# Attention, Hardswish MLP and capacity MoE on one core: Newton steps on GpSimd, output copies on ScalarE, later and denser w_in conversions, the first pair's steps earlier

## The chip, the core and the metric

The kernel runs on one core of a Trainium2 chip (trn2). The metric is the device time in microseconds, as the median of the runs. The engines are TensorE (PE; its weight loads are PEld), VectorE (DVE), ScalarE (ACT), GpSimd (POOL) and SyncE (SP, which here issues the DMAs).

## The reference

Three stages follow one another: attention over 4 batches of 12 heads (448 tokens, head size 64) with RMS-normalised q and k, a Hardswish MLP from 768 to 2048 to 768 over the 1792 tokens, and a mixture of eight experts that fills every expert up to a capacity of 224 tokens.

```python
def rmsnorm(x, g):
    rms = np.sqrt(np.mean(x * x, axis=-1, keepdims=True) + 1e-06)
    return x / rms * g
q_n, k_n = (rmsnorm(q, g_q), rmsnorm(k, g_k))
scores = scale * np.matmul(q_n, k_n.transpose(0, 1, 3, 2))
attn = np.exp(scores - np.max(scores, axis=-1, keepdims=True))
attn_out = np.matmul(attn / (np.sum(attn, axis=-1, keepdims=True) + 1e-09), v)
...
h = x @ w_in                                   # the MLP
x = (h * np.clip(h + 3.0, 0.0, 6.0) / 6.0) @ w_out
...
h = np.maximum(x[mask] @ w1[e], 0.0)           # each of the 8 experts
out[mask] = h @ w2[e]
```

`w_in` and `w_out` come as 64-bit floats; q, k, v and the experts' weights are 32-bit.

## The kernel before

Attention works on pairs of heads, 24 of them, each cut into four chunks of 112 tokens. One pair goes through these functions. `load` and `vload` bring q, k and v. `sums` squares q and k on ACT (`sq`) and adds up the squares on DVE. `invert` turns the mean squares into inverse roots by an integer first guess (lines 240 and 241) and three Newton steps of three small instructions each (lines 243 to 245), all on DVE; it is called once for pair 0, once for pair 1, and from then on once for two pairs together, on tiles of 112x16 or 112x32 elements. `norm` multiplies q and k by the result (`xn`, on GpSimd, but for the very first q). `transp` transposes them on PE and splits them into a high and a low part (`qh`, `ql`, `kh`, `kl`; ACT and DVE). `s1` forms a first score matrix, whose row maxima DVE takes (`mx`); `mt` transposes the maxima, and DVE spreads them (`mr`). `sT` forms the transposed scores by eight matmuls a chunk, and ACT takes exp (`ph`). `av` multiplies with v; at the end of a head DVE reads the row sums (`scol`) and copies the product out of PSUM (`num`, line 374). `normalize` takes the reciprocal on DVE and multiplies on GpSimd (`xq`); `xt` transposes that on PE into the MLP's input (`xh`, `xl`).

In parallel `conv` turns the 64-bit weights into 32-bit ones: one DMA load (`wraw`, two buffers), four DVE instructions over 128x768 elements (`narrow`, lines 134 to 137, into `cv`) and one DMA store, 16 times for `w_in` and 16 times for `w_out`.

The order of all this is written out by hand. Every step gets a place on one scale by `at(t, ...)`, 16 places to a pair, pair i from `t = 16 * i` on; the steps are sorted by place and recorded in that order, and each engine runs its own instructions strictly in that order. So `invert` of a group stands at place 16*g-42, `norm` of pair i at 16*i-38, its transposes at 16*i-30 and 16*i-28, `sT` from 16*i to 16*i+12, `normalize` at 16*i+28 and `xt` at 16*i+33. Between them matmuls of the MLP's first layer (`mlp1_atoms`, line 431) fill PE, from place 117 on, when the first six pairs (batch 0) are through. Its weights are loaded from the converted copy (`win_load`) from place 98 on.

Of the kernel before, what the change touches and what calls it, by code (L numbers as in the profile page):

```python
# [12 lines left out]
AF = mybir.ActivationFunctionType  # L13
OP = mybir.AluOpType
# [7 lines left out]
def kernel(  # L22
# [14 lines left out]
    nc = tc.nc  # L37
# [32 lines left out]
    T_LOAD, T_VLOAD, T_NORM, T_Q, T_K, T_V = -72, -20, -38, -30, -28, 6  # L70
    T_SUMS, T_INV = -50, -42
    T_S1, T_MT = (-24, -20, -16, -12), -7
    T_ST = (0, 4, 8, 12)
    T_AV = ((17, 18, 19.5, 20.5), (22, 23, 24.5, 25.5))
    T_NUM, T_XT, T_MLP = 28, 33, 37
    T_CI, D_CI, T_CO, D_CO, T_CL = 4, 11, 180, 12, 14


    order = ExitStack()
# [158 lines left out]
    def invert(g):  # L238
        ms, y, t = ST[g]
        nc.vector.tensor_scalar(ms, ms, 1.0 / D, 1e-6, op0=OP.mult, op1=OP.add)  # L240
        nc.vector.tensor_scalar(y.bitcast(I32), ms.bitcast(I32), -0.5, 1597463007.0, op0=OP.mult, op1=OP.add)
        for _ in range(3):
            nc.vector.scalar_tensor_tensor(t, y, -0.5, y, op0=OP.mult, op1=OP.mult)
            nc.vector.tensor_tensor(t, t, ms, op=OP.mult)
            nc.vector.scalar_tensor_tensor(y, t, 1.5, y, op0=OP.add, op1=OP.mult)

    def norm(i):
        g = GROUP[i]
# [85 lines left out]
    def av(i, s, n):  # L334
# [29 lines left out]
        num, sc, _ = NUM[i]  # L364
        m = slice(n - QT + 1, n + 1)
        pv = p[:CP, :QT * W].rearrange("p (n w) -> p n w", w=W)
        if SPLIT:
            x = num[:, m, s]
            nc.vector.tensor_scalar(sc[:, s, m], pv[:, :, 128], eps[:CP], None, op0=OP.add)
            nc.vector.tensor_copy(x, pv[:, :, 0:64])  # L370
            nc.vector.tensor_tensor(x, pv[:, :, 64:128], x, op=OP.add)
        else:
            nc.vector.tensor_scalar(sc[:, s, m], pv[:, :, 64], eps[:CP], None, op0=OP.add)
            nc.vector.tensor_copy(num[:, m, s], pv[:, :, 0:64])

    def normalize(i):
        num, sc, xq = NUM[i]
# [248 lines left out]
    def at(t, fn, *args):  # L626
        events.append((t, len(events), fn, args))
# [6 lines left out]

    for i in range(NH // 2):
        t = 16 * i
        at(t + T_LOAD, load, i)
        at(t + T_VLOAD, vload, i)
        g = GROUP[i]
        first = 16 * g[0]  # L640
        at(first + T_SUMS + 4 * (i - g[0]), sums, i)
        if i == g[-1]:
            at(first + T_INV, invert, g)
        at(t + T_NORM, norm, i)
        at(t + T_Q, transp, i, 0)
        at(t + T_K, transp, i, 1)
        at(t + T_V, vsplit, i)
        for c in range(NCH):
            at(t + (T_S1[c] if i else -24 + c), s1, i, c)
            at(t + T_ST[c], sT, i, c)  # L650
            for s in range(2):
                at(t + T_AV[s][c], av, i, s, c)
        at(t + (T_MT if i else -19), mt, i)
        at(t + T_NUM, normalize, i)
        at(t + T_XT, xt, i)
        if (i + 1) % NP == 0:
            at(t + T_MLP, mlp_next, i // NP)
    at(T_LOAD, load_scales)
# [411 lines left out]
    for pi, (t, hfs) in enumerate(passes):  # L1070
# [10 lines left out]
        for f in range(NF):  # L1081
            i, k = divmod(f, QF)
# [139 lines left out]
```

## Time and profile before

| what | value |
|---|---|
| median of 3 runs | 1244.47 us (1239.93 to 1245.07) |
| the profiled execution | 1238.81 us, its span 1237.0 us |
| busy in the span: PE, DVE, ACT, POOL | 1177.1, 807.7, 529.1, 408.2 us |
| mean granted clock of TensorE | 0.98 of full speed |

The profile is of one execution. Busy times of an engine count its instructions; "PEclk" is the clock granted to TensorE in a stretch, 1.00 being 2.4 GHz and 0.50 being 1.2 GHz. A timeline row gives start, duration, engine, line, operation and tiles; in square brackets stands the idle time of the engine ahead of it and what ended that.

### The profile page before, as it was taken

What the parts mean: (1) busy time and instruction counts of PE and PEld (TensorE: products, weight loads), DVE (VectorE), ACT (ScalarE), POOL (GpSimd) and SP (SyncE); (2) the same over time, 40 slices, a digit from 0 to 9 for tenths busy, and PEclk for the clock granted to TensorE, in tenths of its full rate; (3) what the DMA queues carried; (4) which work ended last, traced back from release to release, by engine and by line L of the source; (5) the groups of instructions that cost most, each with busy time, mean ns of one, the idle gap of its engine ahead of it and who ended that gap; (6) DMA issues with size and microseconds to landing.
All of it is one profiled execution on the core that took longest, in us unless ns stands there. A gap on an engine that the chain in (4) does not pass through costs nothing.

```text
span 1237.0 us, 21103 instructions
## 1 busy us (share of the span) xinstructions
PE 1177.1 (95%) x7952; PEld 1008.8 (82%) x7952; DVE 807.7 (65%) x1726; ACT 529.1 (43%) x971; POOL 408.2 (33%) x293
## 2 busy tenths in 40 slices
PE   3899999999999999998998999999998899999997
PEld 2778888888888888887776877777777799999997
DVE  7987967767767866435885466666667565555550
ACT  3543544444454454444773211111112466555650
POOL 2211222223222321012453222222234567666641
PEclk9886999999999999999999999999999899999999
DMA  5563775564554655427986422222234788787731
GB/s 140 151 178 112 198 216 168 164 188 156 179 194 137 194 158 183 145 74 212 325 292 194 119 65 69 64 78 61 71 84 125 220 248 250 238 244 239 227 116 45
DMA packets 221750, 201.69 MB, mean 163 GB/s; under 512 B 19152, under 2 KB 200912, under 8 KB 221648
## 3 DMA queue, kind: packets, MB, share of 16 engines
q1 hardware_dynamic: 218320, 189.33, 51.1%
q0 software_dynamic: 3328, 11.01, 2.9%
q8 instruction: 62, 1.02, 0.3%
q14 instruction: 40, 0.33, 0.1%
HBM read 162.03 MB, written 38.27 MB: 162 GB/s over the span
## 4 chain that ended last, share of the span: by engine, by line
PE 74%; DVE 8%; issue 5%; DMA 3%; POOL 1%; ACT 1%; SPq 0%; POOLq 0%; DVEq 0%; ACTq 0%
PE h L431 17%; PE y L1026 16%; PE av L358 11%; PE y L1174 8%; PE st L318 6%; PE h L1110 5%; PE h L1112 2%; PE rt L837 2%; PE t L273 1%; DVE C L832 1%; PE s L296 1%; DMA gr<-g_dr 1%; DMA we_s<-in_moe_w_dram 1%; PE t L390 1%; PE h L562 1%
## 5 line engine op out<-in xcount | busy, mean ns | idle before, releaser
L358 PEld LDWEIGHTS av<-vv,ph 112*112 112x112 f32 x1536 | 178.6, 186 | 12.5 <-issue 8.5
L358 PE MATMUL av<-vv,ph 112*112 112x66 f32 x1536 | 183.3, 267 | 0.0
L329 ACT ACTIVATE ph<-st 112x448 f32<-112x448 f32 x192 | 93.8, 541 | 140.0 <-PE st L318 139.7
L431 PE MATMUL h<-xh,wh 128*128 128x448 f32 x384 | 152.6, 397 | 0.0
L970 POOL TENSOR_TENSOR g2l<-gr,g2h 128x512 fp32r<-128x512 f32 x60 | 78.7, 1313 | 209.1 <-ACT g2h L968 157.3
L431 PE MATMUL h<-xh,wl 128*128 128x448 f32 x384 | 142.5, 371 | 0.0
L299 DVE TENSOR_REDUCE mx<-s 112x1 f32<-112x448 f32 x192 | 109.3, 612 | 50.7 <-PE s L296 50.6
L431 PE MATMUL h<-xl,wh 128*128 128x448 f32 x384 | 142.1, 370 | 0.0
L112 POOL TENSOR_TENSOR wel<-we_s,weh 128x768 fp32r<-128x768 f32 x60 | 120.6, 2015 | 57.8 <-ACT weh L111 46.3
L112 DVE TENSOR_TENSOR wel<-we_s,weh 128x768 fp32r<-128x768 f32 x68 | 90.2, 1334 | 69.6 <-ACT weh L111 59.3
L111 ACT ACTIVATE weh<-we_s 128x768 fp32r<-128x768 f32 x128 | 105.8, 841 | 69.3 <-DMA we_s<-in_moe_w_dram 51.3
L112 POOL TENSOR_TENSOR wl<-win_v,wh 128x768 fp32r<-128x768 f32 x32 | 60.9, 1903 | 223.3 <-ACT wh L111 209.7
L1026 PE MATMUL y<-woh,g2l 128*128 128x512 f32 (+1 forms) x448 | 128.7, 348 | 1.0 <-POOL g2l L970 1.0
L1026 PE MATMUL y<-woh,g2h 128*128 128x512 f32 (+1 forms) x448 | 127.3, 347 | 0.0
L968 ACT ACTIVATE g2h<-gr 128x512 fp32r<-128x512 f32 x60 | 37.9, 631 | 209.0 <-PE y L1026 159.3
L1026 PE MATMUL y<-wol,g2h 128*128 128x512 f32 (+1 forms) x448 | 126.4, 346 | 0.0
L1110 PE MATMUL h<-xe,weh 128*128 128x448 f32 x384 | 121.1, 377 | 2.2 <-DVE xe L1061 2.2
L1112 PE MATMUL h<-xe,wel 128*128 128x224 f32 x384 | 92.8, 269 | 0.0
L1174 PE MATMUL y<-weh,hl 128*112 128x384 f32 x256 | 86.4, 338 | 0.0
L1174 PE MATMUL y<-weh,hh 128*112 128x384 f32 x256 | 86.3, 337 | 0.0
L1174 PE MATMUL y<-wel,hh 128*112 128x384 f32 x256 | 86.3, 337 | 0.0
L431 PEld LDWEIGHTS h<-xh,wh 128*128 128x128 f32 x384 | 72.5, 189 | 13.3 <-issue 8.3
(235 smaller groups left out, 2386.2 us busy)
## 6 DMA issues: line engine op xcount, KB each, us to landing
we_s<-in_moe_w_dram SPq DMA_DIRECT2D x128, 384.0 KB, 4.4
win_v<-w SPq DMA_DIRECT2D x64, 384.0 KB, 3.9
g_dr<-g SPq DMA_DIRECT2D x64, 224.0 KB, 2.9
gr<-g_dr SPq DMA_DIRECT2D x52, 256.0 KB, 2.9
wraw<-in_moe_w_in_dram SPq DMA_DIRECT2D x16, 768.0 KB, 6.9
wraw<-in_moe_w_out_dram SPq DMA_DIRECT2D x16, 768.0 KB, 7.1
gr<-g_dr SPq DMA_DIRECT2D x48, 224.0 KB, 4.2
w<-cv SPq DMA_DIRECT2D x16, 384.0 KB, 3.1
```

Source lines behind the costliest of these rows:

```text
L111: nc.scalar.activation(hi, raw, AF.Copy)
L112: eng.tensor_tensor(lo, raw, hi.bitcast(F32), op=OP.subtract)
L299: mx = nc.vector.tensor_reduce(MX[i][:, s, c:c + 1], pp[s][:CP, :S], axis=AX.X, op=OP.max)
L318: nc.tensor.matmul(pp[s][:CP, :S], a[r], b[r], start=(n == 0), stop=(n == len(todo) - 1))
L329: nc.scalar.activation(e, pp[s][:CP, :S], AF.Exp)
L358: nc.tensor.matmul(p[:CP, o:o + W], PP[i, s, c][0][:, qs], vv[:, s, c, 64:], start=(c == 0), stop=(c == NCH - 1))
L431: nc.tensor.matmul(p[:, :S], w[:, c], x[:, c], start=(n == 0), stop=(n == 3 * NC - 1))
L970: eng.tensor_tensor(gl, g, gh.bitcast(F32), op=OP.subtract)
L1026: nc.tensor.matmul(pp[hf][:, :COLS[hf].stop - COLS[hf].start], a[:, f % QF], w[:, COLS[hf]], start=(f == 0 and n == 0), stop=(f == NF - 1 ...
L1110: mm = [lambda: nc.tensor.matmul(p[:, :4 * CP], wh[:, fo], x.rearrange("d k t -> d (k t)"), start=(c == 0), stop=(c == NC - 1), skip_group ...
L1112: lambda: nc.tensor.matmul(p[:, :2 * CP], wl[:, fo], x[:, 0], start=False, stop=False, skip_group_check=True)]
L1174: nc.tensor.matmul(p[:CP, :HW], a[:, f, tk], w[:, o], start=(f == 0 and n == 0), stop=(f == FB - 1 and n == 2))
```

## The change

Four things are changed.

1. In `invert` the Newton steps leave DVE for GpSimd. DVE keeps the two instructions of the first guess. GpSimd first multiplies the mean squares by -0.5, and a step is four instructions there instead of three: 1 + 3 x 4 = 13 in place of 9.
2. The copy of the product out of PSUM (`num`) goes from DVE to ACT.
3. The `w_in` conversions start at place 36 instead of 4, and stand 9 places apart instead of 11.
4. For pair 0 alone, `vload`, `vsplit`, `sT`, `av`, `normalize` and `xt` stand 17 places earlier.

```diff
-    T_CI, D_CI, T_CO, D_CO, T_CL = 4, 11, 180, 12, 14
+    T_CI, D_CI, T_CO, D_CO, T_CL = 36, 9, 180, 12, 14
...
         nc.vector.tensor_scalar(y.bitcast(I32), ms.bitcast(I32), -0.5, 1597463007.0, op0=OP.mult, op1=OP.add)
+        nc.gpsimd.tensor_scalar(ms, ms, -0.5, None, op0=OP.mult)
         for _ in range(3):
-            nc.vector.scalar_tensor_tensor(t, y, -0.5, y, op0=OP.mult, op1=OP.mult)
-            nc.vector.tensor_tensor(t, t, ms, op=OP.mult)
-            nc.vector.scalar_tensor_tensor(y, t, 1.5, y, op0=OP.add, op1=OP.mult)
+            nc.gpsimd.tensor_tensor(t, y, y, op=OP.mult)
+            nc.gpsimd.tensor_tensor(t, t, ms, op=OP.mult)
+            nc.gpsimd.tensor_scalar(t, t, 1.5, None, op0=OP.add)
+            nc.gpsimd.tensor_tensor(y, y, t, op=OP.mult)
...
-            nc.vector.tensor_copy(num[:, m, s], pv[:, :, 0:64])
+            nc.scalar.activation(num[:, m, s], pv[:, :, 0:64], AF.Copy)
...
         t = 16 * i
+
+        u = t if i else t - 17
         at(t + T_LOAD, load, i)
-        at(t + T_VLOAD, vload, i)
+        at(u + T_VLOAD, vload, i)
...
-        at(t + T_V, vsplit, i)
+        at(u + T_V, vsplit, i)
...
-            at(t + T_ST[c], sT, i, c)
+            at(u + T_ST[c], sT, i, c)
             for s in range(2):
-                at(t + T_AV[s][c], av, i, s, c)
+                at(u + T_AV[s][c], av, i, s, c)
         at(t + (T_MT if i else -19), mt, i)
-        at(t + T_NUM, normalize, i)
-        at(t + T_XT, xt, i)
+        at(u + T_NUM, normalize, i)
+        at(u + T_XT, xt, i)
```

On PE, from the transpose of pair 0's maxima on (`t<-ident,mx`), before, `st` being the transposed scores, `s` the first scores and `t<-ident,xn` the transposes of pair 1's q and k:

```order
L305 MATMUL t<-ident,mx_107 128x112
L273 MATMUL t<-ident,xn_216 128x112 x4
L273 MATMUL t<-ident,xn_218 128x112 x4
L296 MATMUL s_278<-kh,qh 112x448
L296 MATMUL s_279<-kh,qh 112x448
L296 MATMUL s_294<-kh,qh 112x448
L296 MATMUL s_295<-kh,qh 112x448
L318 MATMUL st<-qh,kh 112x448 x2
```

and with the change:

```order
L307 MATMUL t<-ident,mx_107 128x112
L320 MATMUL st<-qh,kh 112x448 x2
L320 MATMUL st<-qh,kl 112x448 x2
L320 MATMUL st<-ql,kh 112x448 x2
L320 MATMUL st<-mr,minus 112x448 x2
L275 MATMUL t<-ident,xn_226 128x112 x4
L320 MATMUL st<-qh,kh 112x448 x2
L320 MATMUL st<-qh,kl 112x448 x2
```

Pair 0's transposed scores now stand ahead of pair 1's transposes and first scores, chunk by chunk; from 174 matmuls on the two orders are the same.

On DVE at the start of the program, from the last instruction of pair 0's first guess on, before (the Newton steps stand in full once, `xn` is the first multiplication of `norm`):

```order
L241 TENSOR_SCALAR st_1_129<-st_1_128 112x16
L243 SCALAR_TENSOR_TENSOR st_1_130<-st_1_129 112x16
L244 TENSOR_TENSOR st_1_130<-st_1_130,st_1_128 112x16
L245 SCALAR_TENSOR_TENSOR st_1_129<-st_1_130,st_1_129 112x16
...
L256 TENSOR_TENSOR xn_152<-ld_q,st_1_129 112x2x4x64
L236 TENSOR_REDUCE st_1_156<-sq 112x8 x2
```

and with the change:

```order
L241 TENSOR_SCALAR st_1_129<-st_1_128 112x16
L258 TENSOR_TENSOR xn_156<-ld_q,st_1_129 112x2x4x64
L236 TENSOR_REDUCE st_1_162<-sq 112x8 x2
L287 SCALAR_TENSOR_TENSOR ql<-t,gq_72,qh 128x448
L287 SCALAR_TENSOR_TENSOR kl<-t,gk,kh 128x448
```

The nine instructions of each group have left DVE, and the first multiplication now waits for another engine.

On GpSimd, the queue with the change from the second group of two pairs (pairs 4 and 5) on; the steps stand in full once. Before, only the `xn` and `xq` rows stood there:

```order
L242 TENSOR_SCALAR st_2_466<-st_2_466 112x32
L244 TENSOR_TENSOR st_2_468<-st_2_467 112x32
L245 TENSOR_TENSOR st_2_468<-st_2_468,st_2_466 112x32
L246 TENSOR_SCALAR st_2_468<-st_2_468 112x32
L247 TENSOR_TENSOR st_2_467<-st_2_467,st_2_468 112x32
...
L258 TENSOR_TENSOR xn_594<-ld_q,st_2_467 112x2x4x64
L258 TENSOR_TENSOR xn_596<-ld_k,st_2_467 112x2x4x64
L258 TENSOR_TENSOR xn_758<-ld_q,st_2_467 112x2x4x64
L258 TENSOR_TENSOR xn_760<-ld_k,st_2_467 112x2x4x64
L381 TENSOR_TENSOR xq<-num,scol 112x512
```

Each group's 13 instructions stand right ahead of that group's `xn`, and an `xq` of an earlier pair behind them.

## Rows read from the trace of the kernel before

**Rows 1.** Busy time of each engine in four stretches of the span; the columns are stretch, its length, then PE, PEld, DVE, ACT and POOL busy with their counts, the granted clock, the DMA share and GB/s.

```profile
0.00:60.00 60.00, 37.15 (x244) 28.82 (x245) 50.45 (x124) 24.20 (x44) 12.74 (x20) 0.94 0.51 143
60.00:140.00 80.00, 74.72 (x557) 64.37 (x558) 66.73 (x142) 35.47 (x70) 15.89 (x15) 0.81 0.57 158
140.00:550.00 410.00, 409.67 (x2969) 345.17 (x2968) 285.46 (x583) 194.06 (x372) 95.14 (x69) 1.00 0.55 169
550.00:700.00 150.00, 139.30 (x728) 110.59 (x728) 93.72 (x143) 82.19 (x149) 51.97 (x34) 0.99 0.74 230
```

**Rows 2.** What PE waited for in the first 140 us: us in total, times, longest.

```profile
PE t L273 <- DVE xn L256: 10.0, 1, 10.0
PE t L390 <- POOL xq L379: 5.7, 5, 1.6
PE t L305 <- DVE mx L299: 5.3, 1, 5.3
```

**Rows 3.** Groups of DVE instructions in the first 140 us: count, then busy us and mean ns of one, then idle time ahead of them.

```profile
L136 DVE SCALAR_TENSOR_TENSOR cv<-wraw,cv 128x768 int32<-128x768 int32 x10 | 9.6, 960 | 0.2
L137 DVE SCALAR_TENSOR_TENSOR cv<-wraw,cv 128x768 int32<-128x768 int32 x10 | 9.5, 952 | 0.2
...
L134 DVE TENSOR_SCALAR cv<-wraw 128x768 f32<-128x768 f32 x10 | 5.8, 582 | 0.0
L135 DVE TENSOR_SCALAR cv<-cv 128x768 int32<-128x768 int32 x10 | 5.6, 560 | 0.2
L374 DVE COPY num<-av 112x256 f32<-112x256 f32 x12 | 5.0, 413 | 0.0
...
L243 DVE SCALAR_TENSOR_TENSOR st<-st 112x32 f32<-112x32 f32 (+1 forms) x18 | 3.4, 186 | 0.6
```

**Rows 4.** The timeline of the start: pair 0's inverse roots and normalisation, pair 1's, the maxima of pair 0 and the first transposed scores.

```profile
7.20 0.18 DVE L241 TENSOR_SCALAR st<-st 112x16 int32<-112x16 int32 x1
7.42 0.17 DVE L243 SCALAR_TENSOR_TENSOR st<-st 112x16 f32<-112x16 f32 x1
...
9.30 0.69 DVE L256 TENSOR_TENSOR xn<-ld_q,st 112x512 f32<-112x512 f32 x1
9.35 1.54 POOL L256 TENSOR_TENSOR xn<-ld_k,st 112x512 f32<-112x512 f32 x1 [7.83 <-DVE st L245]
...
13.67 0.17 DVE L243 SCALAR_TENSOR_TENSOR st<-st 112x16 f32<-112x16 f32 x1
...
15.43 4.33 DVE L299 TENSOR_REDUCE mx<-s 112x1 f32<-112x448 f32 x8
15.65 1.04 POOL L256 TENSOR_TENSOR xn<-ld_q,st 112x512 f32<-112x512 f32 x1 [4.75 <-issue]
...
19.82 0.45 PE L305 MATMUL t<-ident,mx 112*128 112x112 f32 x1 [5.30 <-DVE mx L299]
...
24.24 0.58 PE L318 MATMUL st<-qh,kh 64*112 64x448 f32 x2
...
24.61 0.58 PE L318 MATMUL st<-qh,kl 64*112 64x448 f32 x2
```

**Rows 5.** The smallest GpSimd instructions of the program, in groups of one form; the last number is the mean ns of one.

```profile
L200 POOL MEMSET vv<- 112x16 f32 x2 | 0.2, 176 | 0.0
L744 POOL IOTA ji<- 128x40 int32 x1 | 0.2, 167 | 0.0
```

**Rows 6.** Timelines of GpSimd and of DVE around one normalisation in the middle of attention (first GpSimd's row, then DVE's).

```profile
241.46 3.28 POOL L256 TENSOR_TENSOR xn<-ld_q,st 112x512 f32<-112x512 f32 x1 [10.10 <-PE s L296]
...
241.15 0.95 DVE L136 SCALAR_TENSOR_TENSOR cv<-wraw,cv 128x768 int32<-128x768 int32 x1
242.02 0.95 DVE L112 TENSOR_TENSOR wl<-win_v,wh 128x768 fp32r<-128x768 f32 x1
242.88 0.95 DVE L137 SCALAR_TENSOR_TENSOR cv<-wraw,cv 128x768 int32<-128x768 int32 x1
243.75 1.15 DVE L299 TENSOR_REDUCE mx<-s 112x1 f32<-112x448 f32 x2
```

**Rows 7.** Stretches of 4 us, with the columns of rows 1.

```profile
80.00:84.00 4.00, 2.21 (x14) 1.05 (x10) 3.97 (x11) 1.95 (x4) 2.79 (x3) 1.00 0.83 226
84.00:88.00 4.00, 3.63 (x20) 3.64 (x21) 3.93 (x7) 0.54 (x1) 0.31 (x1) 0.50 0.18 51
...
116.00:120.00 4.00, 4.00 (x23) 3.31 (x21) 1.78 (x3) 0.98 (x2) 1.53 (x2) 0.50 0.90 270
...
136.00:140.00 4.00, 2.40 (x24) 2.03 (x21) 4.00 (x10) 4.00 (x8) 2.36 (x2) 1.00 0.73 176
```

**Rows 8.** Timeline rows that mark places: the transpose of pair 0's result (place 33), DVE at pair 4's kl (place 36) with the copy of `num` and what follows it, DVE at pair 5's xl (place 113), and the first matmul of the MLP.

```profile
55.48 0.60 PE L390 MATMUL t<-ident,xq 112*128 112x112 f32 x4 [1.26 <-POOL xq L379]
...
61.32 0.68 DVE L285 SCALAR_TENSOR_TENSOR kl<-t,gk,kh 128x448 fp32r<-128x448 f32 x1 [0.17 <-ACT kh L282]
...
62.05 0.41 DVE L374 COPY num<-av 112x256 f32<-112x256 f32 x1
62.38 0.55 DVE L134 TENSOR_SCALAR cv<-wraw 128x768 f32<-128x768 f32 x1
...
142.31 0.61 DVE L392 TENSOR_TENSOR xl<-t,xh 128x448 fp32r<-128x448 f32 x1
...
144.24 0.45 PE L431 MATMUL h<-xh,wh 128*128 128x448 f32 x1
```

## The prediction

> **What bounds the kernel now.** I first cut the span into stretches [rows 1]. From 140 to 550 us PE is busy 409.67 of 410 us at full clock: there DVE (285 of 410), ACT and GpSimd only have to keep pace, and moving work among them gains nothing. The first 140 us are different. PE is idle 22.9 us in the first 60 and 5.3 in the next 80, and in those 80 its mean granted clock is 0.81: with two levels, 2.4 and 1.2 GHz, that is 0.38 x 80 = 30 us at the lower one, or 15 us of PE work lost. DVE is busy 50.5 of 60 and 66.7 of 80. So the ramp, before MLP matmuls come to fill PE at 144 us [rows 8], is where the change can act, and DVE is the engine to look at. The waits of PE agree [rows 2]: 10.0 us for the first xn and 5.3 us for pair 0's maxima, both down to DVE, and 5.7 us in five waits for xq. The 4 us stretches show how DVE and clock hang together [rows 7]: at 80 to 84 DVE is full and PE busy only 2.21; from 84 the clock is at 1.2 GHz, and by 116 to 120 PE is full and DVE down to 1.78 of 4. A late DVE makes PE idle, a PE that idled is then slow, and DVE waits for it. It isn't a fixed rule: 136 to 140 has 2.40 of PE and the clock stays.
>
> **The change part by part.** I count DVE's instructions up to two marks, using the order and the places of the table: pair 4's kl (61.32 us, place 36) and pair 5's xl (142.31 us, place 113) [rows 8].
>
> Newton steps: nine instructions take 1.9 us of DVE (7.42 to 9.30; 13.67 to 15.43 gives 1.8) [rows 4]. Up to the first mark stand four groups, up to the second six. Pair 0's isn't a saving, since everything there waits for its result; three groups x 1.9 = 5.7 us go ahead of the first mark, two x 1.9 = 3.8 between the marks.
>
> Copies of num: 0.33 us from start to start (62.05 to 62.38) [rows 8]; two ahead of the first mark, ten between: 0.7 and 3.3 us. On ACT, busy 35.5 of 80 us [rows 1], they lie beside DVE's work; if that cover were gone they would cost the same 0.3 to 0.5 us each, ahead of xq.
>
> Conversions: one is 0.96 + 0.95 + 0.58 + 0.56 = 3.05 us of DVE [rows 3]. By the places, three stood ahead of the first mark and none does now: 9.2 us off DVE. Between the marks there were seven, now nine: 6.1 us more. Their DMAs move with them: a wraw load still stands 14 places ahead of its conversion, on SP it comes one place behind the store that waits for the buffer's last reader, so its order holds, and the third conversion (place 54) is long done when the first MLP weights are loaded (place 98). I cost this at nothing; after 140 us the denser ones lie under a full PE.
>
> Sum on DVE: 5.7 + 0.7 + 9.2 = 15.6 us ahead of the first mark; 3.8 + 3.3 - 6.1 = 1.0 between.
>
> The price on GpSimd: 13 small instructions in a chain. The trace of before has no small arithmetic there. From below, a memset of 112x16 and an iota of 128x40 take 0.18 and 0.17 us [rows 5], so 13 x 0.17 = 2.2 us; from above, a multiplication of 16 to 32 times the elements takes 1.04 us [rows 4], so 13.5 us. Dependent instructions on DVE start 0.21 us apart although each lasts 0.17 [rows 4]. I take 0.25, nearest to the small ones, so 3.3 us for a chain. Pair 0's chain lies bare: 3.3 - 1.9 = 1.4 us lost. Pair 1's doesn't: DVE is free at once for the eight maxima, which in before start at 15.43 behind those nine instructions, so mt and the first transposed scores come no later. From pairs 4 and 5 on 12 places lie between the chain's start and the transposes.
>
> GpSimd also shares something with DVE. The xn at 241.46 took 3.28 us instead of 1.04; three DVE instructions with two SBUF inputs stood back to back, and 1.0 us after the last one's end at 243.75 xn was done [rows 6]. So it was held for all three. The same shows at 9.35: 1.54 us beside DVE's xn [rows 4]. The Trainium skill, "SBUF — State Buffer", section "Who interferes with whom", says so: a DVE instruction with two SBUF inputs or in a two-port mode and a GpSimd instruction that reads SBUF exclude each other for a whole instruction; the rows agree. For this change it means that a chain beside a conversion (places 54 to 57 hold both) grows by up to the conversion's 3.05 us, to 6.4. With two xn of 1.04 that makes 8.4 us, within 12 places at about a microsecond each (77 places from 61.32 to 142.31), so I cost it at nothing and leave it to a rival.
>
> Pair 0's earlier steps: no work is added, but PE does 32 matmuls of its scores ahead of pair 1's. They run at the low rate there: two start 0.37 us apart (24.24, 24.61) [rows 4], so 16 x 0.37 = 6.0 us. DVE can wait for that between 0 and 6.0 us; I take 2, since DVE has pair 2's and 3's squares to add meanwhile. In return pair 0's multiplication with v fills PE where it waited.
>
> So DVE reaches the first mark 15.6 - 1.4 - 2 = 12.2 us earlier, the second another 1.0: 13.2. The order from place 36 on is as before, PE's load between the marks too, so I keep the waits and the low-clock stretches there as they are. Behind, PE is the bound and nothing is given back. Against the profiled execution's own time: 1238.8 - 13.2 = 1225.6 us. The three runs of before lie 1.1 to 6.3 above it; I add 2.4, a little under half, for a time of **1228**.
>
> A sentence on another rule: the Trainium skill, "GPSIMD Engine Reference", section "4.1 Engine selection", advises against this move, since elementwise work with two inputs is about twice as slow on GpSimd. Twice DVE's 0.17 would be 0.34 us for one, an estimate from that page: 4.4 us a chain, 1.1 more than I take, in three bare chains 3.4 us, and the sum would be 1231. No row shows it at this size.
>
> **The rivals.**
>
> (a) The clock stays up. With DVE less late, PE idles less, and the 30 us at 1.2 GHz after 60 us shrink. DVE's idle time there is 80 - 66.7 = 13.3 us [rows 1], nearly all while PE was slow; if it goes, 1228 - 13 = 1215. For it: the fall at 84 follows a stretch in which DVE was full. Against it: between the marks DVE's load falls by 1.0 us only.
>
> (b) xq comes late. Every second xq now stands in GpSimd's queue behind 13 instructions and two xn, six places after the chain may start and five ahead of xt. PE already waits for xq five times [rows 2]. If each of the three chains between places 54 and 118 holds it for its full 3.3 us, that is 10 us: 1238. For it: held chains of 6.4 + 2.1 us are longer than six places. Against it: the reciprocal on DVE comes earlier too.
>
> (c) The small instructions are slow, and the kernel gets slower. The first three chains (pairs 0, 1, and 2 with 3) lie bare or nearly so: each 0.1 us more on one of 39 instructions costs 3.9 us. The gain of 13.2 is gone at 0.25 + 13.2/39 = 0.59 us each; with 1.04 us, the time of a whole xn, the loss is 39 x 0.79 = 31 us: 1259. Against it: 0.17 and 0.18 us for the smallest instructions [rows 5]. For it: none of those depends on the one ahead of it.
>
> **How the numbers follow.** Forecast 0.52, (a) 0.20, (b) 0.20, (c) 0.08. The forecast's own range: a small instruction of 0.17 instead of 0.25 is worth 3, PE's lateness 0 to 6 is -2 to +4, the run's distance from the profile -2 to +4: some 1220 to 1236. For 8 in 10 I reach down to where (a) is mostly in, 1209, and up past (b), 1241; (c) and the far end of (a) stay out. A measurement of this kernel can tell about 0.5% from no change, 6.2 us, so faster is below 1238.3: the forecast, (a), and half of (b), 0.82. Within it lies the other half of (b), 0.10; slower is (c), 0.08.
>
> **What would show it.** In the profile after, the first MLP matmul should stand near 131 instead of 144.24, pair 0's xt near 40 instead of 55.48, pair 4's kl near 49. GpSimd's Newton rows should start about 0.25 us apart; at 0.6 (c) holds. A PE that waits for xq more than 5.7 us in all speaks for (b); a granted clock above 0.9 from 50 to 130 us speaks for (a). Idle PE between 140 and 550 would mean that the forecast's base, a full PE behind the ramp, no longer stands.

## The result and the profile after

The kernel became slower: a median of 1262.8 us in 4 runs (1250.71 to 1268.34), beside 1244.34 us before, a ratio of 1.0142 with a 95% interval of 1.0098 to 1.0185. The forecast was 1228 us. The profiled execution took 1268.34 us, its span 1266.5: 5.5 us above its median, while that of before (1238.81) lies 5.5 below its own. So the two traces lie 29.5 us apart where the medians differ by 18.

The stretches, after, with the columns of [rows 1]:

```profile
0.00:60.00 60.00, 39.20 (x221) 29.06 (x221) 34.70 (x72) 23.48 (x44) 22.01 (x69) 0.83 0.33 96
60.00:140.00 80.00, 64.64 (x449) 55.62 (x450) 54.41 (x99) 30.75 (x63) 27.18 (x41) 0.75 0.45 128
140.00:550.00 410.00, 407.93 (x2871) 344.51 (x2872) 274.04 (x488) 200.02 (x390) 126.06 (x161) 0.96 0.57 174
```

DVE's work did fall, 50.45 to 34.70 us and 66.73 to 54.41 in the first two stretches, but PE got through 670 instructions there instead of 801, at a lower clock. Past 140 us PE is as good as full, as forecast. What PE waited for in the first 144 us, after:

```profile
PE t L392 <- POOL xq L381: 12.0, 3, 5.5
PE t L275 <- DVE xn L258: 11.9, 1, 11.9
PE t L275 <- POOL xn L258: 4.3, 2, 2.8
PE t L307 <- DVE mx L301: 3.4, 1, 3.4
```

and, of the same view of before, the line that [rows 2] leaves out:

```profile
PE t L273 <- POOL xn L256: 1.8, 1, 1.8
```

The wait for pair 0's maxima shrank from 5.3 to 3.4 us, but that for xq doubled (12.0 instead of 5.7), and that for GpSimd's xn grew from 1.8 to 4.3. The places of [rows 8] after (pair 0's xt, pair 4's kl, the first MLP matmul), from the timelines of PE and DVE:

```profile
47.26 1.01 PE L392 MATMUL t<-ident,xq 112*128 112x112 f32 x4 [1.38 <-POOL xq L381]
...
66.97 0.68 DVE L287 SCALAR_TENSOR_TENSOR kl<-t,gk,kh 128x448 fp32r<-128x448 f32 x1 [0.45 <-ACT kh L284]
...
171.43 0.72 PE L433 MATMUL h<-xh,wh 128*128 128x448 f32 x1
```

Pair 0's xt is 8 us earlier (forecast: 15), pair 4's kl 5.7 us later (forecast: 12 earlier), and the first MLP matmul 27.2 us later, which is nearly all of the 29.5. So the loss lies in the ramp. The timeline of GpSimd for the chain of pairs 6 and 7, what DVE did beside it, and PE's next transpose, after:

```profile
88.97 0.53 POOL L242 TENSOR_SCALAR st<-st 112x32 f32<-112x32 f32 x1 [11.05 <-DVE st L241]
...
90.45 1.57 POOL L246 TENSOR_SCALAR st<-st 112x32 f32<-112x32 f32 x1
92.10 0.25 POOL L247 TENSOR_TENSOR st<-st,st 112x32 f32<-112x32 f32 x1
92.43 0.93 POOL L244 TENSOR_TENSOR st<-st 112x32 f32<-112x32 f32 x1
...
95.84 1.04 POOL L258 TENSOR_TENSOR xn<-ld_q,st 112x512 f32<-112x512 f32 x1
96.84 1.35 POOL L258 TENSOR_TENSOR xn<-ld_k,st 112x512 f32<-112x512 f32 x1
98.16 1.58 POOL L381 TENSOR_TENSOR xq<-num,scol 112x512 f32<-112x512 f32 x1
...
90.92 0.95 DVE L136 SCALAR_TENSOR_TENSOR cv<-wraw,cv 128x768 int32<-128x768 int32 x1
...
92.32 0.95 DVE L137 SCALAR_TENSOR_TENSOR cv<-wraw,cv 128x768 int32<-128x768 int32 x1
...
99.80 1.01 PE L392 MATMUL t<-ident,xq 112*128 112x112 f32 x4 [5.47 <-POOL xq L381]
```

The 13 instructions take 6.8 us here: an instruction of 0.29 us takes 1.57 and one of 0.24 takes 0.93 while a conversion's two-input instructions run on DVE. Then come two xn, and xq, which DVE's reciprocal had released at 93.6, starts at 98.16. PE stands idle for 5.47 us. Not every group is like this one. PE's rows for the transpose of pair 0's maxima, the first transposes of pairs 2 and 4, and the xq behind the chain of pairs 8 and 9, with GpSimd's next xq behind the chain of pairs 4 and 5, after:

```profile
19.83 0.45 PE L307 MATMUL t<-ident,mx 112*128 112x112 f32 x1 [3.42 <-DVE mx L301]
...
32.80 1.01 PE L275 MATMUL t<-ident,xn 112*128 112x112 f32 x4 [2.75 <-POOL xn L258]
...
61.40 0.60 PE L275 MATMUL t<-ident,xn 112*128 112x112 f32 x4 [1.50 <-POOL xn L258]
...
139.84 1.01 PE L392 MATMUL t<-ident,xq 112*128 112x112 f32 x4 [5.19 <-POOL xq L381]
...
76.86 1.06 POOL L381 TENSOR_TENSOR xq<-num,scol 112x512 f32<-112x512 f32 x1 [9.41 <-ACT num L376]
```

Behind the chains of pairs 2 and 3 and of pairs 4 and 5 it is xn itself that PE waits for, 2.75 and 1.50 us. No xq is held there: the next one comes at 76.86, after GpSimd has itself waited 9.41 us for `num`. An xq held by a chain shows only behind those of pairs 6 and 7 and of pairs 8 and 9, where PE waits 5.47 and 5.19 us for it. Stretches of 5 us around PE's wait of 5.47 us, after:

```profile
95.00:100.00 5.00, 0.20 (x1) 0.21 (x2) 2.32 (x4) 0.55 (x2) 4.49 (x6) 0.63 0.81 240
100.00:105.00 5.00, 5.00 (x29) 5.00 (x28) 1.49 (x2) 1.04 (x2) 0.40 (x1) 0.50 0.01 3
```

GpSimd is nearly full, PE does next to nothing and DVE works 2.32 of 5 us; then PE, back from its idle time, runs at 1.2 GHz, and DVE works 1.49 of 5. From the windows up to the first MLP matmul, one can account for DVE's time:

| kernel | first MLP matmul | DVE busy until then | DVE idle until then | granted clock 60 to 140 |
|---|---|---|---|---|
| before | 144.24 | 121.4 | 22.8 | 0.81 |
| after | 171.43 | 107.7 | 63.7 | 0.75 |

The 13.7 us of work are gone, as the forecast had it; 40.9 us of idle time came in their place.

### The profile page after: what moved, and what is told of

Read it like the earlier page. It is cut to its first block, busy times and chain, and to the rows that moved or that the text cites. A ratio compares the mean times of both kernels' runs of the same rounds, so it can differ in the third digit from the quotient of the medians.

```text
span 1266.5 us, 21133 instructions
## 1 busy us (share of the span) xinstructions
PE 1199.4 (95%) x7952; PEld 1028.1 (81%) x7952; DVE 776.0 (61%) x1561; ACT 545.1 (43%) x1019; POOL 462.7 (37%) x462
## 4 chain that ended last, share of the span: by engine, by line
PE 71%; DVE 6%; DMA 5%; issue 4%; ACT 1%; POOL 1%; SPq 0%; POOLq 0%; DVEq 0%; ACTq 0%
PE y L1030 16%; PE h L433 16%; PE av L360 10%; PE y L1178 8%; PE st L320 6%; PE h L1114 5%; PE h L1116 2%; DMA gr<-g_dr 2%; PE rt L841 2%; PE t L275 1%; DMA wo_s<-wo 1%; PE s L298 1%; DVE C L836 1%; DVE gl L463 1%; PE h L564 1%
## 5 line engine op out<-in xcount | busy, mean ns | idle before, releaser
L360 PEld LDWEIGHTS av<-vv,ph 112*112 112x112 f32 x1536 | 190.7, 197 | 13.5 <-issue 9.1
L360 PE MATMUL av<-vv,ph 112*112 112x66 f32 x1536 | 195.3, 278 | 0.0
L331 ACT ACTIVATE ph<-st 112x448 f32<-112x448 f32 x192 | 93.7, 542 | 107.3 <-PE st L320 107.0
```

The lines of the kernel that those rows point to most:

```text
L331: nc.scalar.activation(e, pp[s][:CP, :S], AF.Exp)
L360: nc.tensor.matmul(p[:CP, o:o + W], PP[i, s, c][0][:, qs], vv[:, s, c, 64:], start=(c == 0), stop=(c == NCH - 1))
```

## The experiments

Every kernel gets a line in this table; "busy" and "idle" are DVE's up to the first MLP matmul, in the one profiled execution. The medians of before in the later sets of runs were 1242.5 to 1246.5, so ratios are to be compared, not medians. The first MLP matmul isn't the whole story: from it to the end of the span it takes 1093 us in before and between 1092 and 1102 in the others, so up to 9 us more than in before come behind it. A trace is one execution, and those of after, f2, j2 and k1 are of the slowest execution of their kernel, that of e1 of its fastest.

| kernel | ratio to before (95%) | first MLP matmul | busy / idle | clock 60 to 140 |
|---|---|---|---|---|
| e1 change, Newton on DVE | 1.0109 (1.0065 to 1.0153) | 149.02 | 117.5 / 31.5 | 0.79 |
| e2 Newton on GpSimd alone | 1.0145 (1.0069 to 1.0221) | 167.90 | 112.1 / 55.8 | 0.80 |
| e3 pair 0 alone | 1.0046 (1.0010 to 1.0082) | 147.34 | 122.1 / 25.2 | 0.83 |
| e4 conversions alone | 1.0026 (1.0005 to 1.0048) | 146.73 | 120.0 / 26.7 | 0.79 |
| e5 copies alone | 0.9988 (0.9955 to 1.0020) | 148.65 | 121.6 / 27.1 | 0.87 |
| f3 change, one step | 0.9964 (0.9932 to 0.9997) | 145.53 | 107.0 / 38.5 | 0.74 |
| f4 change, chain earlier | 1.0023 (0.9996 to 1.0049) | 148.36 | 109.8 / 38.6 | 0.85 |
| j1 change, xq on DVE | 1.0076 (1.0041 to 1.0111) | 150.45 | 110.7 / 39.7 | 0.83 |
| h1 change, much filler | 1.0157 (1.0118 to 1.0196) | 164.95 | 107.0 / 58.0 | 0.92 |
| f2 e1, much filler | 1.0026 (0.9990 to 1.0063) | 156.54 | 117.5 / 39.0 | 0.94 |
| h2 f4, much filler | 1.0018 (0.9990 to 1.0046) | 144.96 | 109.9 / 35.0 | 0.98 |
| h3 hidden chain alone, much filler | 1.0050 (1.0022 to 1.0077) | 151.74 | 117.3 / 34.4 | 1.00 |
| j3 f4, little filler | 1.0027 (0.9995 to 1.0059) | 139.50 | 108.5 / 31.0 | 0.94 |
| f1 before, much filler | 0.9975 (0.9949 to 1.0001) | 143.37 | 121.6 / 21.8 | 1.00 |
| j2 before, little filler | 0.9914 (0.9882 to 0.9946) | 139.76 | 121.3 / 18.5 | 1.00 |
| k1 j2 and copies | 0.9898 (0.9869 to 0.9926) | 139.91 | 118.4 / 21.6 | 1.00 |
| j4 before, ten conversions cut | 0.9828 (0.9781 to 0.9876) | 123.67 | 98.2 / 25.5 | 1.00 |
| k2 before, three conversions cut | 0.9912 (0.9887 to 0.9937) | 137.97 | 116.6 / 21.3 | 0.85 |

### The four parts by themselves

**e1**, the change with the Newton steps back on DVE:

```diff
-            nc.gpsimd.tensor_tensor(t, y, y, op=OP.mult)
...
+            nc.vector.scalar_tensor_tensor(t, y, -0.5, y, op0=OP.mult, op1=OP.mult)
```

> The changed kernel with its Newton steps back on DVE (the other three edits stay). Theory A (the chain of 13 dependent GpSimd instructions, 4.3 us alone and 6.9 us beside a conversion in the trace of the changed kernel, makes xn and xq late, PE idles up to 5.5 us in a place and runs at 1.2 GHz after it): the loss of 18.5 us goes and the 13.2 us of the prediction's sum less the 9.5 us of Newton steps remain, so some 1235 to 1242 us, waits of PE for xq under 6 us in the first 144 us. Theory B (the new order of pair 0 and of the conversions lets PE run ahead and idle, whoever does the Newton steps): it stays at 1255 to 1265 us.

**e2**, the kernel before with the Newton steps on GpSimd and nothing else:

```diff
-            nc.vector.scalar_tensor_tensor(t, y, -0.5, y, op0=OP.mult, op1=OP.mult)
...
+            nc.gpsimd.tensor_tensor(t, y, y, op=OP.mult)
```

> The kernel of before with the Newton steps on GpSimd and nothing else. Theory A: slower than before by most of what the change lost, 1255 to 1270 us, with PE waits for xq of 3 to 6 us behind every chain and a mean granted clock under 0.8 between 60 and 140 us. Theory B: DVE gains 9.5 us in the ramp and the time is 1235 to 1245 us.

**e3**, the kernel before with pair 0's steps earlier:

```diff
+        u = t if i else t - 17
-            at(t + T_ST[c], sT, i, c)
+            at(u + T_ST[c], sT, i, c)
```

> The kernel of before with pair 0's steps 17 places earlier and nothing else. Theory A: nothing that loses, 1238 to 1246 us; pair 0's xt comes at 40 to 45 us instead of 55.5, but DVE's work ahead of place 36 is the same and still sets that place. Theory B: 1250 us or more, with PE idle time in the stretch after pair 0's xt and a lower clock behind it.

**e4**, the kernel before with the later, denser conversions:

```diff
-    T_CI, D_CI, T_CO, D_CO, T_CL = 4, 11, 180, 12, 14
+    T_CI, D_CI, T_CO, D_CO, T_CL = 36, 9, 180, 12, 14
```

> The kernel of before with the w_in conversions from place 36 on and 9 places apart, and nothing else. Theory A: DVE gains 9.2 us ahead of place 36 and loses 6.1 between 36 and 113, so 1236 to 1244 us. Theory B: the denser conversions hold DVE and GpSimd up between 60 and 140 us, and the time is 1250 us or more.

**e5**, the kernel before with the copies of `num` on ACT:

```diff
-            nc.vector.tensor_copy(num[:, m, s], pv[:, :, 0:64])
+            nc.scalar.activation(num[:, m, s], pv[:, :, 0:64], AF.Copy)
```

> Only the copies of num on ScalarE. The three parts other than the Newton steps together (e1) cost 1.1%, pair 0 alone 0.5%, conversions alone 0.3%. If the parts simply add, the copies are worth +0.3% (1246 to 1249 us beside 1244); theory that DVE's time in the ramp isn't what paces it: within 0.3% of before, and the 1.1% is then a product of the parts together. Theory of the forecast (DVE's time counts): 0.33 x 12 = 4 us less, 0.997.

The Newton steps alone make the first MLP matmul 23.7 us later, of the change's 27.2, and take as long as the whole change. In e2, against before, DVE's kl of pairs 2, 4, 6 and 8 (35.65, 68.96, 105.98 and 149.18 instead of 32.94, 61.32, 94.23 and 130.28) fall back by 2.7, 4.9, 4.1 and 7.2 us more with each group, and PE's waits for xq behind the chains of pairs 6 and 7 and of pairs 8 and 9 are 7.18 and 7.23 us. But the three other parts are no gain either: pair 0 and the conversions are slightly slower each, and of the copies the interval allows both 0.45% less and 0.2% more. The parts' ratios don't add up to that of the whole (e1 and e2 together would be 2.5%). And e1's median lies only 0.3 points below that of the change, which the intervals don't tell from nothing, though its trace, the fastest of its four executions, has the first MLP matmul 22 us earlier. Of the expectations, theory A held for e2; e1 lies between its two theories, e3 and e4 above theory A and below theory B, and the interval of e5 excludes only the +0.3%.

In e4, pair 4's kl is 6.3 us earlier (55.05), as the forecast has it for the conversions; pair 5's still is (70.71 instead of 76.90), pair 7's no longer (111.37 instead of 110.90). Three stretches of 4 us in e4 show where:

```profile
76.00:80.00 4.00, 2.48 (x10) 1.17 (x10) 4.00 (x9) 0.76 (x2) 0.92 (x2) 0.81 0.00 0
80.00:84.00 4.00, 3.53 (x17) 3.07 (x18) 2.29 (x5) 0.77 (x2) 1.01 (x1) 0.50 0.92 259
...
92.00:96.00 4.00, 4.00 (x23) 3.68 (x24) 0.55 (x2) 0.00 (x0) 0.00 (x0) 0.50 0.79 225
```

DVE's timeline in e4, at two of its waits there:

```profile
82.61 0.56 DVE L134 TENSOR_SCALAR cv<-wraw 128x768 f32<-128x768 f32 x1 [1.71 <-DMA w<-cv]
...
96.81 1.16 DVE L299 TENSOR_REDUCE mx<-s 112x1 f32<-112x448 f32 x2 [4.12 <-PE s L296]
```

DVE is full and PE idles 1.5 of 4 us, PE then is slow and DVE idles 4.12 us for it: the picture of [rows 7], once more and 4 us earlier. And a conversion waits 1.71 us until the store of an earlier one has read its buffer `cv`.

### The chain: shorter, earlier, or without xq behind it

**f3**, the change with one Newton step instead of three (5 small instructions instead of 13; two steps are left out, so the inverse roots are less exact):

```diff
-        for _ in range(3):
+        for _ in range(1):
             nc.gpsimd.tensor_tensor(t, y, y, op=OP.mult)
```

> The changed kernel with one Newton step in place of three (it leaves out two steps, so the inverse roots are coarser): 5 GpSimd instructions a chain instead of 13, some 1.7 us instead of 4.3. Theory A (the length of the chain makes xn and xq late): the PE waits of 5 us for xq are gone, and the time comes down by most of the 10 to 16 us that separate the changed kernel from the one with its steps back on DVE: 1245 to 1255 us. Rival (it is GpSimd's place, the semaphore to it and back, not the length): 1258 to 1268 us.

**f4**, the change with the sums and the inverse roots six places earlier:

```diff
-    T_SUMS, T_INV = -50, -42
+    T_SUMS, T_INV = -56, -48
```

> The changed kernel with the squares' sums and the inverse roots 6 places earlier (the table's numbers -56 and -48 instead of -50 and -42), so that a chain has 18 instead of 12 places ahead of the transposes, and 12 instead of 6 ahead of xq. Theory A: the chain of 4.3 to 6.9 us is covered, PE waits for xq under 6 us in the first 144 us, 1240 to 1252 us. Rival (the exclusion between DVE and GpSimd costs DVE as much as it gained, wherever the chain stands): no change, 1255 to 1268 us.

**j1**, the change with xq of pairs 0 to 8 on DVE:

```diff
-        nc.gpsimd.tensor_tensor(xq, num, sc[...
+        (nc.vector if i < 9 else nc.gpsimd).tensor_tensor(xq, num, sc[...
```

> The whole change, with the multiplication xq of pairs 0 to 8 on VectorE instead of GpSimd, so that it no longer stands behind the chain and the two xn in GpSimd's queue. Theory that the loss is xq held in that queue (rival (b) of the prediction): TensorE's waits for xq (17 us up to 145 us in the changed kernel) fall below 4 us, the first MLP matmul moves from 171 to 145 to 152, the time to 1238 to 1248. Rival, that the chain makes xn and with it the transposes late: the waits move to xn, first MLP matmul stays past 160, time 1253 to 1265.

(Of the 17 us named there the trace has 12.0, in three waits.) All three bring the first MLP matmul back by 21 to 26 us, and the time by 0.7 to 1.8 points. f3 gained more than expected (1239.48 us), f4 lies in the range of theory A, and j1 has its theory's first MLP matmul, but a time (1250.69) between the two theories. So the length and place of the chain, with what queues behind it, carry the loss of the ramp. DVE at the kl of pairs 2, 4, 6 and 8, each the first of two pairs that share a chain, from the timeline of the changed kernel:

```profile
39.01 0.68 DVE L287 SCALAR_TENSOR_TENSOR kl<-t,gk,kh 128x448 fp32r<-128x448 f32 x1 [0.46 <-ACT kh L284]
...
109.67 0.68 DVE L287 SCALAR_TENSOR_TENSOR kl<-t,gk,kh 128x448 fp32r<-128x448 f32 x1 [0.46 <-ACT kh L284]
...
149.71 0.68 DVE L287 SCALAR_TENSOR_TENSOR kl<-t,gk,kh 128x448 fp32r<-128x448 f32 x1 [0.46 <-ACT kh L284]
```

and from that of f4:

```profile
35.49 0.68 DVE L287 SCALAR_TENSOR_TENSOR kl<-t,gk,kh 128x448 fp32r<-128x448 f32 x1
...
57.90 0.69 DVE L287 SCALAR_TENSOR_TENSOR kl<-t,gk,kh 128x448 fp32r<-128x448 f32 x1 [0.18 <-ACT kh L284]
...
92.25 0.69 DVE L287 SCALAR_TENSOR_TENSOR kl<-t,gk,kh 128x448 fp32r<-128x448 f32 x1 [0.45 <-ACT kh L284]
...
126.61 0.68 DVE L287 SCALAR_TENSOR_TENSOR kl<-t,gk,kh 128x448 fp32r<-128x448 f32 x1
```

With pair 4's kl at 66.97 (above), the changed kernel lies 3.5, 9.1, 17.4 and 23.1 us behind f4: 3.5, 5.6, 8.3 and 5.7 more with each group. The four chains take 4.2, 4.3, 6.8 and 4.7 us. So a group pays 0.8 to 1.3 times its chain's length. f4 has DVE's sums earlier too; no run has the earlier places without the chain, so their own share isn't known. PE's first transposes of pairs 2 and 4 wait for nothing in f4:

```profile
31.78 0.55 PE L275 MATMUL t<-ident,xn 112*128 112x112 f32 x4
...
54.03 0.55 PE L275 MATMUL t<-ident,xn 112*128 112x112 f32 x4
```

For the chain of pairs 6 and 7, f4's is over before xq is wanted; GpSimd's and PE's rows there:

```profile
78.11 1.76 POOL L258 TENSOR_TENSOR xn<-ld_k,st 112x512 f32<-112x512 f32 x1
81.31 1.06 POOL L381 TENSOR_TENSOR xq<-num,scol 112x512 f32<-112x512 f32 x1 [1.44 <-ACT num L376]
...
82.42 0.97 PE L392 MATMUL t<-ident,xq 112*128 112x112 f32 x4 [0.69 <-POOL xq L381]
```

GpSimd itself waits 1.44 us for `num`, and PE 0.69 instead of 5.47. In j1, PE's waits for xq fall from 12.0 to 3.2 us, and 4.2 for xn stay: the first MLP matmul is 21.0 of the 27.2 us earlier, but the time gains only about half of what was lost (1.0076 instead of 1.0142). So xq in the queue, which rival (b) named, is a large part, and xn late is another.

### The clock: filler for PE

**f1**, the kernel before with repeated matmuls in pairs 0 to 5 (the first matmul of each `av` and `sT` group twice, six matmuls of 448 columns ahead of each `xt`, all overwritten by the real ones; an estimated 21 us of added work):

```diff
+                for _ in range(1 if i < 6 and c == 0 else 0):
+                    nc.tensor.matmul(p[:CP, o:o + W], PP[i, s, c][0][:, qs], vv[:, s, c, 64:], start=True, stop=True)
...
+        for _ in range(1 if i < 6 else 0):
+            for s, r in enumerate(ROWS):
+                nc.tensor.matmul(pp[s][:CP, :S], kh[r, ck], qh[r], start=True, stop=True)
...
+        for _ in range(6 if i < 6 else 0):
+            nc.tensor.matmul(t[:, :S], OPER[i + 1][0][:, 0:128], OPER[i + 1][2], start=True, stop=True)
```

> The kernel of before with extra PE work in the first six pairs: the first matmul of each accumulation in av and in sT is issued twice, and six more matmuls of 448 columns stand ahead of each xt, all overwritten by the real ones. That is some 3.6 us of PE work a pair at full clock, 21 us in all, and no other engine has more to do. Clock theory (the ramp is paced by stretches at 1.2 GHz that follow PE's idle time, not by DVE's sum of work): the clock stays up, the 37 us at 1.2 GHz ahead of 140 us shrink to under 15, and the time is the same or lower, 1228 to 1245 us, although PE does more. Rival (PE's clock is a side show, PE work counts as work): 10 to 21 us slower, 1252 to 1265 us.

**f2**, e1 with the same repeated matmuls (its profiled execution was the slowest of its ten):

```diff
+        for _ in range(6 if i < 6 else 0):
```

> The changed kernel with its Newton steps back on DVE, and the same extra PE work in the first six pairs as in the run on the kernel of before. Clock theory: with the clock up, DVE's 7 us less work in the ramp show at last, 1222 to 1238 us, and the mean granted clock from 60 to 140 us is above 0.9 (0.79 without the extra work). Rival (PE work counts as work): 1260 to 1273 us.

**h1**, the change with them:

```diff
+        for _ in range(6 if i < 6 else 0):
```

> The whole change, with about 21 us of repeated matmuls in pairs 0 to 5 (first matmul of each av and sT group twice, six 448-column matmuls ahead of each xt; the result is unchanged). Theory that the clock's falls multiply the late xq: the six matmuls ahead of xt fill PE while it waits for xq, the granted clock from 60 to 200 us goes above 0.9 (0.75 before), and the time falls by 10 to 20 us in spite of the added work, to 1243 to 1252. Rival, that the chain's own lateness is the loss: the wait is only filled, PE has 21 us more to do, time 1262 to 1285.

**h2**, f4 with them:

```diff
-    T_SUMS, T_INV = -50, -42
+    T_SUMS, T_INV = -56, -48
+        for _ in range(6 if i < 6 else 0):
```

> The whole change with the sums and the inverse roots six places earlier, and the repeated matmuls. Theory: what is left of the late xq in the kernel with the earlier inverse roots (6.6 us of waits, clock 0.85) goes, and it comes below both kernels, 1230 to 1240. Rival (the ramp is paced by its work, not by the clock): 1246 to 1256.

**h3**, e2 with f4's earlier places and with them:

```diff
-    T_SUMS, T_INV = -50, -42
+    T_SUMS, T_INV = -56, -48
+        for _ in range(6 if i < 6 else 0):
```

> The kernel before with Newton steps on GpSimd alone, the sums and inverse roots six places earlier, and the repeated matmuls. Theory: a hidden chain costs nothing, so it is level with or a little below the kernel before with the repeated matmuls (1241.7, 0.9975): 1233 to 1242. Rival (the chain also takes DVE's time by the exclusion of the two engines): 1248 to 1260.

**j2**, the kernel before with the six matmuls ahead of `xt` alone:

```diff
+        for _ in range(6 if i < 6 else 0):
+            nc.tensor.matmul(t[:, :S], OPER[i + 1][0][:, 0:128], OPER[i + 1][2], start=True, stop=True)
```

> The kernel before with only the six repeated 448-column matmuls ahead of the xt of pairs 0 to 5 (some 7 us of added TensorE work at full clock instead of some 21). Theory that the clock paces the ramp: with less filler and a clock still near 1.00 the first MLP matmul comes 5 to 13 us ahead of 144, time 1230 to 1238. Rival, that another engine or a loop through several paces the ramp, and the filler only lies in TensorE's idle and slow time: first MLP matmul within 3 us of 144, time level with the kernel before (1239 to 1246).

**j3**, f4 with those, for pairs 0 to 8:

```diff
-    T_SUMS, T_INV = -50, -42
+    T_SUMS, T_INV = -56, -48
+        for _ in range(6 if i < 9 else 0):
```

> The whole change with sums and inverse roots six places earlier, and the six repeated matmuls ahead of xt alone, for pairs 0 to 8. Clock theory: the stalls past 140 us go too, below both kernels, 1230 to 1238. Rival (a loop through several engines paces it): 1241 to 1248, level with the same kernel with more filler (1245).

**k1**, j2 with the copies on ACT:

```diff
-            nc.vector.tensor_copy(num[:, m, s], pv[:, :, 0:64])
+            nc.scalar.activation(num[:, m, s], pv[:, :, 0:64], AF.Copy)
+        for _ in range(6 if i < 6 else 0):
```

> The kernel before with the six repeated matmuls ahead of the xt of pairs 0 to 5 (0.9914 by themselves), and the copies of num on ScalarE. Theory that VectorE's time sets the ramp once the clock is up: the copies take 12 x 0.33 = 4 us more off it, first MLP matmul near 136, 0.988 (1226 to 1230). Rival, that the copies gain nothing because ScalarE has num behind exp and xq waits for it: level with the filler alone, 0.991 to 0.994.

My theory at h1 was that the late xq costs so much because the clock falls after it. The theory fell: the filler brings the clock of 60 to 140 us from 0.75 to 0.92, and the time stays at 1.0157. PE's transposes of the xq of pairs 2 to 5 in h1:

```profile
98.48 0.60 PE L399 MATMUL t<-ident,xq 112*128 112x112 f32 x4 [2.22 <-POOL xq L386]
117.78 0.57 PE L399 MATMUL t<-ident,xq 112*128 112x112 f32 x4
137.65 0.69 PE L399 MATMUL t<-ident,xq 112*128 112x112 f32 x4 [3.76 <-POOL xq L386]
157.74 0.55 PE L399 MATMUL t<-ident,xq 112*128 112x112 f32 x4
```

In the changed kernel they stand at 99.80, 119.01, 139.84 and 162.06. At a clock of 0.92 and with more to do PE arrives at the same places 1 to 4 us earlier. I read this so that the round through DVE's first guess, GpSimd's chain and PE sets the pace there, and much of the slow clock lies inside its waits; the filler's own work weighs against what the clock gives, and the changed kernel was not run with the little filler of j2.

In the kernel before, with no chain in the round, a little filler does gain: j2 is 0.86% faster, and three times the filler (f1) gives most of that back. j2's trace has the first MLP matmul 4.5 us earlier, but it is of its slowest execution, at 1240.19 us, so it doesn't show where the median's gain lies. In e1 the filler takes back most of the loss (f2: 1.0026 instead of 1.0109). The copies of k1 add nothing that can be measured. Both beat the two kernels at hand, with 1229.78 and 1231.3 us.

With the chain hidden no filler reaches that (h2, j3). h3, without the three other parts, lies in its rival's range: 0.5% slower than before and 0.75 points above f1 with the same filler, so even the hidden chain isn't free. Whether the exclusion of the two engines or the earlier places cost this isn't separated; DVE's `narrow` instructions take as long there as in f1 (0.95 us at line 137 in both). As for the other expectations, the clock theory held in f1 and (to 0.3 us) in j2, and the rival in h1 and j3; f2 and k1 lie between their two and h2 1 us below its rival's range. j3's first MLP matmul is as early as j2's, but it takes 1102 us from there to the end of its span, which I haven't explained.

### DVE's time in place

**j4**, the kernel before with the first ten w_in conversions cut to their first instruction (the other three are left out, so these weights aren't converted):

```diff
+    thin = [10]
...
+        thin[0] -= 1
+        if thin[0] >= 0:
+            return (lambda: nc.vector.tensor_scalar(v, hi.bitcast(F32), 2.0 ** -112, None, op0=OP.mult),) + (lambda: None,) * 3
```

> The kernel before, with the first ten w_in conversions cut to their first instruction (0.56 us instead of 3.05; the other three are left out, so the converted weights are wrong): some 25 us less for VectorE in the first 140 us, and no DMA, wait or order changed. Forecast's theory that VectorE's time is what the ramp costs: kl of pair 4 some 9 us earlier (52), the first MLP matmul 20 us or more earlier (under 125), time under 1228. Rival, that VectorE's time isn't what paces the ramp past pair 4: the first MLP matmul within 8 us of 144, time 1236 to 1245.

**k2**, the same for the first three only, those ahead of pair 4's kl:

```diff
+    thin = [3]
```

> The kernel before with only the first three w_in conversions (those ahead of pair 4's kl) cut to their first instruction, so 7.5 us less for VectorE at the places which the change empties, and nothing added later (the converted weights of those are wrong). Theory that VectorE's time counts where it stood: kl of pair 4 at 54 to 55, the first MLP matmul at 135 to 138, 0.993 to 0.996. Then the conversions of the change lose their gain by being denser between 60 and 145 us. Rival, that this time was cover for another wait: kl of pair 4 early as in the kernel with the conversions alone (55.05), but the first MLP matmul within 3 us of 144 and 0.998 to 1.002.

DVE works 23.2 us less up to the first MLP matmul in j4, and that comes 20.6 us earlier, as the theory had it, though pair 4's kl, at 57.56, is only 3.8 us earlier and not 9; its stretch from 60 to 140 us:

```profile
60.00:140.00 80.00, 77.32 (x674) 66.22 (x671) 68.09 (x154) 43.50 (x85) 20.78 (x18) 1.00 0.68 192
```

In k2 7.5 us of work are gone (the table's 4.8 less, since DVE is five instructions further by then), the first MLP matmul is 6.3 us earlier, as the theory had it, and the time 0.9% shorter. So DVE's time does set the ramp of the kernel before, as the forecast said, when it is simply gone. e4 empties the same places (pair 4's kl at 55.05, in k2 at 55.31) and gives it all back by pair 7.

## Why the prediction was wrong

**What held.** The ramp is where the change acts, PE is full behind it, and DVE's work is what it costs in the kernel before (j4, k2). DVE's work fell by 13.7 us up to the first MLP matmul, against 16.6 counted. The clock of PE and DVE's lateness hang together as [rows 7] showed.

**The step that failed first** is "From pairs 4 and 5 on 12 places lie between the chain's start and the transposes ... so I cost it at nothing and leave it to a rival". It failed in two ways. For pairs 4 and 5 the 12 places were too short: PE waited 1.50 us for xn itself. For pairs 2 and 3 it waited 2.75 us (1.84 before); the sum has no term for that chain, though rival (c) calls it bare or nearly so. Behind the chains of pairs 6 and 7 and of pairs 8 and 9 it was the next instruction in GpSimd's queue: xq is recorded 6 places after the chain and wanted by PE's transposes 5 places on, and PE takes its work in order, so it waited 5.47 and 5.19 us. In the queue of pairs 4 and 5 no xq stands so close, since the change moved pair 0's ahead. Four groups paid 3.5 to 8.3 us each, 23.1 in all up to pair 8's kl (after against f4). Rival (b) named the place and mechanism of the late xq, but priced three groups at 3.3 us, 10 in all: it took a chain's bare length, where the conversion beside it (6.8 us) and the two xn ahead of xq count too, and it left out the late xn (PE's 4.3 us of waits). The first two chains, where the sum charged 1.4 us, cost nothing at the transpose of pair 0's maxima: 19.83 us after, 19.82 before.

**The price of a chain** was a little low: in the changed kernel its instructions start 0.22 to 0.38 us apart (16 elements a partition: 13 in 3.9 us; 32: 13 in 4.2 to 4.3), against 0.25 taken. The Trainium skill, "GPSIMD Engine Reference", section "4.1 Engine selection", calls two-input elementwise work on GpSimd about twice as slow; the estimate made from it, 4.4 us a chain, is close to what the chains beside no conversion took, 3.9 to 4.3 us. Rival (c) asked for 0.59 us to lose the gain. That break-even stood on three bare chains; here the kernel loses at 0.33, with four later chains on the path. That the measured 1262.8 us lie near the 1259 of (c) is luck, since its condition wasn't met.

**Beside a conversion** a chain of 6.4 us was expected from [rows 6], and it took 6.8. The rule of the Trainium skill, "SBUF — State Buffer", section "Who interferes with whom", agrees with these rows: the instructions that took longest (1.57 and 0.93 us) overlap DVE's two-input ones of lines 136 and 137. Beside the one-input ones of the same conversion (0.56 us) two small instructions took 0.53 and 0.57 us, which the page's case of a two-port mode would explain; no row shows in which mode those ran.

**The second step that failed** is "I keep the waits and the low-clock stretches there as they are". With the chain hidden (f4) DVE has 11.6 us less to do than before, and 15.8 us more idle time; the first MLP matmul is 4 us later. In parts:
- Conversions: net 9.2 - 6.1 = 3.1 us of DVE's time, measured 0.26% slower. The gain at pair 4 is real, 6.3 of the 9.2 us (e4; 6.0 in k2); moving three conversions into 60 to 140 us, with two more there than before, gave it back in a stall of PE, low clock and a wait of 1.71 us for a store. "Their DMAs move with them ... at nothing" missed that store. How the rest divides isn't settled.
- Pair 0: a loss of 2 us was taken; alone it puts pair 4's kl 5.4 us later (66.72) and is 0.46% slower. Its xt comes 13 us earlier (42.36), but pair 1's 5.6 later (74.31 instead of 68.74): pair 0's steps only passed those that all later pairs need.
- Copies: 4.0 us of DVE's time, and nothing that could be measured in e5 or k1.
- Why the three together lose more (e1: 1.1%) than by themselves, and more than f4 (0.2%), which has them and the hidden chain, stays open.

**Rival (a)** went the other way, 0.75 instead of above 0.9. Its price was doubtful too: of DVE's 13.3 us of idle time from 60 to 140 us some 10, and not nearly all, lie in those 4 us stretches of before whose clock is below 1.00. And a clock kept up by filler goes with a gain of 0.86% in the kernel before with a little of it (j2) and of 0.25%, not clear of noise, with much (f1), and with no gain in the changed one with much (h1).

## What to carry to other kernels

When work leaves a busy engine for an idle one, count what stands behind it in the idle engine's queue, and ask how soon that is wanted, not only when the moved work's own result is. A dependent chain of small instructions on the way between engines cost about its whole length here in each of four rounds, and starting it earlier took most of that back, however idle its engine looks on average. Time on the limiting engine counts where it is removed; where it is only moved within the ramp, expect the waits to move with it.

## What the runs showed of the hardware

An estimated 7 us of needless matmuls ahead of a wait made the kernel before 0.9% faster (j2), and the granted clock from 60 to 140 us was 1.00 instead of 0.81. The clock isn't the whole of it: f1, with three times the filler, has the same 1.00 and a gain that isn't clear of noise, and in the changed kernel that filler raised the clock to 0.92 without a gain. Small GpSimd instructions of 16 to 32 elements a partition take 0.20 to 0.29 us, and the next dependent one starts about 0.08 us after that, so their size hardly counts: twice the elements (32 instead of 16) made a chain 4.2 us instead of 3.9.
